# Two weight loads move from SyncE's to ScalarE's DMA queue, and the written-out order of operations is replaced (attention and mixer-MLP layer, one core)

## The chip, the cores and the metric

The kernel runs on one core of a Trainium2 chip. Five engines work side by side, each on its own stream of instructions: TensorE (PE: matrix products and transposes into PSUM; PEld in the profile is its weight load), VectorE (DVE), ScalarE (ACT), GpSimd (POOL) and SyncE (SP, which issues DMAs here). They meet through semaphores. Transfers run on 16 DMA engines.

The metric is the device time of one execution in microseconds. Three runs of the kernel before gave 193.75, 194.11 and 195.71 us; the median is 194.11.

## The reference

The input is x, [1, 2048, 448] in bf16. Two blocks follow one another, each with a residual around it:

```python
h  = x + A_ref(layernorm(x))      # attention, 16 heads of 28
h2 = h + B_ref(layernorm(h))      # token shift + MLP

# A_ref: qkv = x @ wqkv; each position attends to itself and the 7 positions
#   2, 4, ... 14 before it (window 8, dilation 2); softmax; @ wo
# B_ref: h = gelu(layernorm(x) @ w1); its four groups of 112 channels are shifted
#   by +1, -1, +2, -2 positions; hs = shifted @ w2; x1 = x + hs
#   return x1 + gelu(layernorm(x1) @ w3) @ w4        # 448 -> 1792 -> 448
```

## The kernel before, in words

**Tiling.** The 2048 positions are 16 tiles of 128 rows, in xin, one DMA buffer for the whole input. Attention works on four blocks t of 512 positions, the MLP on five units u of 2, 4, 4, 4 and 2 tiles. For a block t the phases are N1 (layernorm), A1 (q and k, transposed to channels x positions), V (values), A2 and S (scores and softmax), A3 and O (weighted sum and wo, with the residual), B1 and M (second layernorm, w1, gelu). For a unit u: B2 (shift and w2) and T (third layernorm), W3 (w3, gelu) and B3 (w4, output). A name such as A11 is phase A1 of block 1.

**Products in pairs.** 448 channels are four chunks that overlap. Most products are made by `duo`, which runs two results at once, one on the upper 64 rows of the array and one on the lower; so the profile has them as 64*128. One operation of the program is such a group of products.

**Layernorm and transposes.** For each tile VectorE makes statistics (bn_stats, bn_aggr into mv), ScalarE or GpSimd makes the reciprocal root (rs_x, then rs_y; `rstd`), and a normalization writes lntm. The transposed lntm, actT, comes from TensorE with copies by ScalarE or VectorE for the attention blocks, and from a transposing DMA on SP for M and W3. The helper chains SP's DMAs around these: a transposing DMA waits for all loads and copies issued since the last one, and the next copies wait for it (`arrange`, lines 205 to 210). For scores, VectorE multiplies q with shifted k into qk_r (phase A2, line 750) and the weights with a mask into bd_r (phase A3); both are long operations on 128x4096 and 80x2048 elements.

**What sets the order.** The program makes 891 operations, numbered as they are made. ORDER (lines 19 to 50) is a permutation of these numbers, written out in the file; each engine's stream is what ORDER has of its operations, in that sequence. The position in ORDER relative to operations of other engines has no effect of its own: semaphores carry the dependences. OTHER lists operations that take their alternative engine (a copy on VectorE for ScalarE or the other way, the product pb in S on GpSimd for VectorE). Waits are made from the dependences (`_emit_plan`); the first goes with the instruction, further ones are instructions of their own (line 992).

**The loads.** `load_x` (lines 428 to 429) and `load_rows` (431 to 434) make the loads; they are operations 8 to 38. All are issued on SP, in the order in which they are made (lines 459 to 462 hold this order per engine). 8, 9 and 10 are the first three loads of x (tile 0, tile 1, tiles 2 and 3); 12 and 13 are the two halves of the q/k part of wqkv, 128 x 2 x 896 elements each, both needed by the first product of A10; 14 and 15 are x tiles 4 to 7; 16 and 17 the v part; 18 and 19 the rest of x; then wo, w1, w2, w3 (35, 36) and w4 (37, 38).

**Operations that the prediction names.** On ScalarE: 60 and 61, 65 and 66, 72 and 73 are the pairs rs_x and rs_y of tile 0, tile 1 and tiles 2 and 3; 11 is a small Exp on a constant, made among the loads (line 440). 101 and 104 are copies of actT in A10, 127 and 134 copies in A10, 230 a copy of actT in A11, 378 one of vt in V2, 408, 528 and 534 copies of actT in A32 and A33, 161 the product pb of S0.

Within a phase the order of instructions on SP before is: x0, x1, x2, wqk (two), x4, x6, wv (two), x8, x12, wo, w1, w2, then copies of vt into vw (V blocks) mixed with w3, transposes for M0 and M1, one vw copy, w4 first half, one vw copy, w4 second half, the transpose for the first W3 unit, two vw copies, the transpose for M2, and so on.

Of the kernel before, what the change touches and what calls it, by code (L numbers as in the profile page):

```python
# [16 lines left out]
POWER = {'N1': 'aaaa', 'B1': 'aaaa', 'B2': 'apapp'}  # L17
RESIDUAL = 'ttvv'
ORDER = """
# [30 lines left out]
"""  # L50
OTHER = """
104 127 196 197 199 402 408 411 519 525 528 582 583
"""
FULL = (4,)
FILL = (1, 1, 0, 0)
# [226 lines left out]
def bass_sequential_preLN__sliding_local_dilated__mixer_s_mlp__prompt_kernel(  # L282
    nc, A_x, A_wqkv, A_wo, B_x, B_w1, B_w2, B_w3, B_w4, out,
):
    _, SEQ, D = A_x.shape
# [30 lines left out]
    with ExitStack() as es:  # L316
# [43 lines left out]
        def arv(off, parts, n):  # L360
            return AR[0:parts, off:off + n]

        wqkv_s = arv(A_W, 128, 4 * 1344).rearrange("p (c n) -> p c n", c=4)
# [29 lines left out]
        def act(out_ap, in_ap, func, **kw):  # L393
            table = {ACT.Exp: "exp", ACT.Ln: "exp", ACT.Gelu_apprx_tanh: "gelu"}.get(func)
            return S.add("act", "activation", table=table, out=out_ap, in_=in_ap, func=func, **kw)
# [15 lines left out]
        def dma(chan, out_ap, in_ap, nbytes, eng="sp", **kw):  # L411
            return S.add(eng, "dma_start", chan=chan, nbytes=nbytes, out=out_ap, in_=in_ap, **kw)
# [15 lines left out]
        def load_x(i, n):  # L428
            return dma("x%d" % i, xin[:, i:i + n, :], xv[:, i:i + n, :], 128 * n * D * 2)

        def load_rows(chan, dst, src, lo, n):

            for h in range(2):
                dma("%s%s" % (chan, "ab"[h]), dst[:, 2 * h:2 * h + 2, :], src[192 * h:192 * h + 256, lo:lo + n].rearrange("(c k) n -> k c n", k=128), 256 * n * 2)

        S.tag = "load"
        for i in range(2):
            load_x(i, 1)
        load_x(2, 2)
        act(zs[:, 0, 0:1], epsilon[:, 0:1], ACT.Exp)  # L440
        load_rows("wqk", wqkv_s[:, :, 0:2 * D], A_wqkv, 0, 2 * D)
        load_x(4, 2)
        load_x(6, 2)
        load_rows("wv", wqkv_s[:, :, 2 * D:3 * D], A_wqkv, 2 * D, D)
        for i in range(8, NTL, 4):
            load_x(i, 4)
# [3 lines left out]
        for k, (to, lo, n) in enumerate(((0, 112, 336), (336, 0, 112), (448, 48, 64))):  # L450
            load_rows("w1%d" % k, w1_s[:, :, to:to + n], B_w1, lo, n)
# [584 lines left out]
```

## Time and profile before

| what | value |
|---|---|
| median of three runs | 194.11 us (193.75 to 195.71) |
| profiled execution: span from its first to its last instruction | 192.0 us |
| the rest of the median, around the span | 2.1 us |
| TensorE busy | 181.2 us, 94% of the span |
| VectorE busy | 129.6 us, 67% |
| ScalarE busy | 133.0 us, 69% |
| GpSimd busy | 29.3 us, 15% |
| TensorE's granted clock | 1.000 |
| 16 DMA engines, hardware queue | 37.1% |

The profiled execution has a span of 192.0 us; what lies around it (launch and end) is not in the span, and is taken as the difference to the median. A line of the profile such as "PE MATMUL ps<-actT,arena 64*128 64x256 bf16 x98" names the engine, the operation, the tile that it writes and those that it reads, its shape and how many there were; all instructions carry line 994, the line that emits them, so one goes by tiles. arena is one large buffer for wqkv, w3, w4, q, k, weights of the attention and the MLP's first result. SPq is SP's queue: a DMA's issue, not its transfer.

### The profile page before, as it was taken

How to read it: one execution, taken by the hardware profiler on the slowest of the kernel's cores; microseconds unless marked ns; L12 is line 12 of the kernel's file. 1: busy time of each engine (PE TensorE's matmuls, PEld its weight loads, DVE VectorE, ACT ScalarE, POOL GpSimd, SP SyncE). 2: the span in 40 equal slices, each digit the busy share in tenths (PEclk: the TensorE clock that was granted, in tenths of full speed). 3: DMA queues.
4: the chain of work that ended last, by engine and by line, in shares of the span. 5: the costliest groups of instructions: out<-in, count | busy, mean ns of one | idle time of the engine just before them, and what ended most of it. 6: DMA issues, size and time to landing. Idle time of an engine off the chain costs nothing.

```text
span 192.0 us, 5741 instructions
## 1 busy us (share of the span) xinstructions
PE 181.2 (94%) x2482; PEld 92.6 (48%) x2482; DVE 129.6 (67%) x229; ACT 133.0 (69%) x310; POOL 29.3 (15%) x63
## 2 busy tenths in 40 slices
PE   6999999999999869969999999999999999999994
PEld 2584533453444333337545444455444544555672
DVE  7899999999999999999876970036988022002203
ACT  4489999999999999998595898860158004731340
POOL 3240000000004000201067000022077700000000
DMA  5998792005504163935905014006200542000111
GB/s 146 353 282 175 194 295 44 14 0 133 133 3 90 23 66 72 319 64 125 113 3 106 8 34 103 0 0 126 58 26 1 109 106 73 0 3 0 51 48 48
DMA packets 30273, 17.04 MB, mean 89 GB/s; under 512 B 18936, under 2 KB 29736, under 8 KB 30248
## 3 DMA queue, kind: packets, MB, share of 16 engines
q1 hardware_dynamic: 30248, 16.68, 37.1%
q8 instruction: 19, 0.31, 0.7%
q14 instruction: 6, 0.05, 0.1%
HBM read 8.04 MB, written 1.84 MB: 51 GB/s over the span
## 4 chain that ended last, share of the span: by engine, by line
PE 67%; DMA 13%; ACT 12%; DVE 3%; SPq 2%; issue 1%; POOL 0%; POOLq 0%; ACTq 0%
PE ps L994 67%; DMA actT<-lntm 7%; DMA arena<-in_B_w_dram 3%; ACT lntm L994 3%; ACT arena L994 3%; DMA vw<-vt 2%; ACT vt L994 2%; SPq L994 2%; DVE bd_r L994 2%; ACT h3T L994 1%; ACT actT L994 1%; ACT xin L994 1%; DVE lntm L994 1%; DVE ost L994 1%; ACT ls L994 1%
## 5 line engine op out<-in xcount | busy, mean ns | idle before, releaser
L994 PE MATMUL ps<-actT,arena 64*128 64x256 bf16 (+1 forms) x756 | 68.7, 329 | 2.2 <-DMA actT<-lntm 1.7
L994 ACT ACTIVATE h3T<-ps 128x512 bf16<-128x512 f32 (+1 forms) x70 | 30.3, 525 | 40.1 <-PE ps L994 40.0
L994 PEld LDWEIGHTS ps<-actT,arena 64*128 64x128 bf16 x756 | 35.4, 94 | 31.6 <-DMA actT<-lntm 2.1
L994 PE MATMUL ps<-arena,h3T 64*128 64x448 bf16 (+2 forms) x434 | 44.4, 343 | 0.0
L994 ACT ACTIVATE arena<-ps 128x512 bf16<-128x512 f32 (+10 forms) x86 | 40.1, 515 | 3.3 <-PE ps L994 2.5
L994 DVE SCALAR_TENSOR_TENSOR ost<-ps,mrs,arena 128x448 bf16<-128x448 f32 (+1 forms) x17 | 10.7, 652 | 36.5 <-PE ps L994 36.5
L994 DVE TENSOR_TENSOR qk_r<-arena 128x4096 bf16<-128x4096 bf16 (+1 forms) x16 | 32.0, 2016 | 0.4 <-ACT arena L994 0.2
L994 PEld LDWEIGHTS ps<-arena,h3T 64*128 64x128 bf16 (+1 forms) x434 | 23.0, 94 | 18.7 <-issue 0.2
L994 POOL TENSOR_TENSOR arena<-arena,xin 128x448 f32<-128x448 f32 x16 | 17.2, 1088 | 45.0 <-DVE lntm L994 45.0
L994 DVE TENSOR_TENSOR bd_r<-arena,bmask 80x2048 bf16<-80x2048 bf16 x16 | 19.0, 1216 | 1.6 <-PE ps L994 0.9
L994 ACT ACTIVATE actT<-ps 128x512 bf16<-128x512 f32 (+2 forms) x21 | 14.6, 742 | 2.1 <-PE ps L994 2.1
L994 PE MATMUL ps<-actT,w_s 64*128 64x512 bf16 x112 | 13.3, 377 | 1.7 <-DMA actT<-lntm 1.2
L994 PE MATMUL ps<-wo_s,actT 64*128 64x448 bf16 x128 | 14.3, 350 | 0.1
L994 PE MATMUL ps<-arena,actT 64*128 64x448 bf16 x112 | 12.4, 350 | 0.4 <-ACT vt L994 0.4
L994 PE MATMUL ps<-w_s,arena 64*128 64x448 bf16 x112 | 11.6, 350 | 1.0 <-ACT arena L994 0.9
L994 ACT ACTIVATE lntm<-xin,nm 128x448 bf16<-128x448 bf16 x16 | 10.5, 660 | 2.6 <-DVE nm L994 2.6
L994 DVE SCALAR_TENSOR_TENSOR arena<-xin,rs_y,ps 128x448 f32<-128x448 bf16 x16 | 10.3, 672 | 2.2 <-PE ps L994 2.2
L994 DVE TENSOR_SCALAR lntm<-arena,mv,rs_y 128x512 bf16<-128x512 f32 x14 | 10.2, 773 | 2.1 <-POOL rs_y L994 2.0
L994 POOL TENSOR_TENSOR pb<-ls,mx 128x512 bf16<-128x512 f32 x2 | 3.3, 1641 | 52.8 <-ACT mx L994 52.8
L994 DVE BATCH_NORM_STATS2 st<-xin 128x6 f32<-128x448 bf16 x16 | 9.4, 614 | 0.8 <-DMA xin<-in_A_x_dram 0.7
L994 PEld LDWEIGHTS ps<-actT,w_s 64*128 64x128 bf16 x112 | 5.1, 94 | 8.9 <-PE ps L994 1.7
L994 PEld LDWEIGHTS ps<-wo_s,actT 64*128 64x128 bf16 x128 | 5.6, 94 | 6.7 <-PE ps L994 1.4
(73 smaller groups left out, 161.7 us busy)
## 6 DMA issues: line engine op xcount, KB each, us to landing
arena<-in_B_w_dram SPq DMA_DIRECT2D x2, 896.0 KB, 7.3
out_dram<-ost SPq DMA_DIRECT2D x15, 112.0 KB, 1.9
arena<-in_B_w_dram SPq DMA_DIRECT2D x2, 784.0 KB, 5.7
vw<-vt SPq DMA_DIRECT2D x4, 320.0 KB, 4.3
vw<-vt SPq DMA_DIRECT2D x4, 256.0 KB, 4.2
arena<-in_A_wqkv_dram SPq DMA_DIRECT2D x2, 448.0 KB, 4.6
xin<-in_A_x_dram SPq DMA_DIRECT2D x2, 448.0 KB, 7.5
xin<-in_A_x_dram SPq DMA_DIRECT2D x3, 224.0 KB, 5.6
```

The lines of the kernel that those rows point to most:

```text
L994: inst = getattr(eng, meth)(**kw)
```

## The change

`load_rows` gets an argument for the issuing engine, and the two loads of the q/k weights (12, 13) pass "act", so they are issued by ScalarE. ORDER is another permutation of the same 891 operations, and OTHER has other members.

```diff
 OTHER = """
-104 127 196 197 199 402 408 411 519 525 528 582 583
+101 134 161 196 197 198 230 378 402 411 519 525 534 582 583
 """
...
-        def load_rows(chan, dst, src, lo, n):
+        def load_rows(chan, dst, src, lo, n, eng="sp"):
 
             for h in range(2):
-                dma("%s%s" % (chan, "ab"[h]), dst[:, 2 * h:2 * h + 2, :], src[192 * h:192 * h + 256, lo:lo + n].rearrange("(c k) n -> k c n", k=128), 256 * n * 2)
+                dma("%s%s" % (chan, "ab"[h]), dst[:, 2 * h:2 * h + 2, :], src[192 * h:192 * h + 256, lo:lo + n].rearrange("(c k) n -> k c n", k=128), 256 * n * 2, eng)
...
-        load_rows("wqk", wqkv_s[:, :, 0:2 * D], A_wqkv, 0, 2 * D)
+        load_rows("wqk", wqkv_s[:, :, 0:2 * D], A_wqkv, 0, 2 * D, "act")
```

Of ORDER, all of which changes, the first three lines before and after:

```diff
-43 8 7 2 11 0 1 49 44 45 6 9 10 12 5 39 13 40 42 58 59 60 61 63 64 62 70 68 50 51 52 53 54 55 56 57 14 65 66 71 69 67
-72 73 75 77 97 15 98 99 100 102 105 74 76 103 101 41 113 119 104 106 46 212 125 218 126 84 107 214 114 216 129 130 215
-89 86 93 78 87 3 108 133 132 115 116 213 217 16 127 128 17 18 219 131 120 109 110 121 338 220 221 224 122 95 223 47
+5 39 6 0 40 1 43 2 42 41 7 8 58 59 60 11 9 63 64 65 10 68 70 69 71 61 62 66 67 72 73 75 44 84 85 92 89 91 74 49 50 51
+52 53 54 55 56 57 97 99 100 102 105 103 12 13 76 98 101 119 106 113 107 77 78 88 46 87 14 214 212 15 218 216 213 217
+47 104 125 120 215 219 220 221 126 129 108 131 130 121 127 128 133 132 122 123 114 124 109 16 17 18 334 223 222 335
...
```

By engine, where the prediction speaks of it:

- ScalarE begins 60, 11, 65, 61, 66, 72, 73, then 12 and 13 (the two loads), then 98 and 106 (copies of actT). Before it began 11, 60, 61, 65, 66, 72, 73, 98.
- VectorE begins with the clearing of vt and pb, both parts of bmask (42, 41), the clearing of wo_s, and then the statistics. Before, it cleared wo_s first and made the second part of bmask after the normalizations of block 0.
- SP issues x0, x1, x2, x4, x6, wv (two), x8, x12, and then a copy of vt of block 0, which has to wait for V0. wo, w1, w2 and w3 come after that.
- Later on SP: transposes for M0 and M1, the two large vw copies of block 3, the transpose for the first W3 unit, w4 (two), one vw copy, the transpose for M2.
- On TensorE all four operations of the first B3 unit stand before M2; before, two of them did, and two came after it, around O3.

54 rows, old and new, of the table ORDER are left out of this document.

## The prediction

> **What bounds the kernel now.** I read the shares of the engines first, then the engines' busy time by stretch, then the chain that ended last and TensorE's own waits, and last the first 16 us instruction by instruction. On the page and in a table of busy time by stretch (columns: length, PE, PEld, DVE, ACT, POOL with instruction counts, clock, DMA share, GB/s):
>
> ```profile
> span 192.0 us, 5741 instructions
> PE 181.2 (94%) x2482; PEld 92.6 (48%) x2482; DVE 129.6 (67%) x229; ACT 133.0 (69%) x310; POOL 29.3 (15%) x63
> 15.60:68.80 53.20, 50.84 (x901) 23.11 (x897) 52.62 (x65) 52.71 (x136) 2.21 (x1) 1.00 0.40 95
> 96.00:188.80 92.80, 92.73 (x983) 48.10 (x984) 37.80 (x83) 46.66 (x93) 19.26 (x21) 1.00 0.19 44
> ```
>
> From 15.6 to 68.8 us (attention) VectorE is busy 52.62 of 53.20 us and ScalarE 52.71: both are full, and whatever arrives late there stays late. From 96 to 188.8 (the MLP) TensorE is busy 92.73 of 92.80 and nothing else matters. So the end is set by when that last, full stretch begins, and by TensorE's gaps before it. The clock is 1.00 throughout. The chain between (start, length, what) and TensorE's waits from 60 to 97 us:
>
> ```profile
> 68.82 5.27 DMA actT<-lntm
> ...
> 76.09 6.49 DMA arena<-in_B_w_dram
> ...
> 82.60 3.06 DMA actT<-lntm
> ...
> 90.60 5.43 DMA actT<-lntm
> ...
> 96.07 92.72 PE ps L994 x981
> ```
> ```profile
> PE ps L994 <- DMA actT<-lntm: 2.9, 3, 1.7
> PE ps L994 <- ACT arena L994: 1.9, 4, 0.7
> PE ps L994 <- ACT rs_x L994: 0.3, 1, 0.3
> ```
>
> The middle is SP's queue in series: transpose for M1 (68.82), then the two w4 loads (to 82.58), then the transpose for the first W3 unit (to 85.67), then two vw copies, then the transpose for M2 (90.60). TensorE waits 5.1 us in all here; the longest wait, 1.7, is for the first W3 unit.
>
> Now the beginning, in order of time:
>
> ```profile
> 0.81 1.34 SPq L994 DMA_DIRECT2D xin<-in_A_x_dram  x3
> 2.19 0.98 SPq L994 DMA_DIRECT2D arena<-in_A_wqkv_dram  x2
> 3.08 0.61 DVE L994 BATCH_NORM_STATS2 st<-xin 128x6 f32<-128x448 bf16 x1
> 6.23 0.30 ACT L994 ACTIVATE rs_x<-mv,epsilon 128x2 f32<-128x2 f32 x1 [1.03 <-DVE mv L994]
> 6.67 1.61 ACT L994 ACTIVATE actT<-ps 128x512 bf16<-128x512 bf16 x3
> 7.42 0.41 DVE L994 TENSOR_REDUCE bmask<-ls 80x32 bf16<-80x256 bf16 x1
> 8.19 5.81 PE L994 MATMUL ps<-actT,arena 64*128 64x256 bf16 x98 [0.24 <-issue]
> 13.84 0.63 PE L994 MATMUL ps<-ident,lntm 64*128 64x64 bf16 x32
> 15.59 2.28 DVE L994 TENSOR_TENSOR qk_r<-arena 128x4096 bf16<-128x4096 bf16 x1
> ```
>
> SP issues the q/k weights at 2.19. The first q/k product starts at 8.19, when the actT copies (6.67 to 8.28) are nearly done as well.
>
> **The change part by part: the loads.** In ScalarE's new order operations 12 and 13 stand behind 60, 11, 65, 61, 66, 72 and 73, that is behind the rs_x row at 6.23 and the rs_y that follows it. Does ScalarE's queue issue a DMA before the instructions ahead of it have been released? The wait instructions (line 992, first and last start at the end of each row) and the landing times bear on it:
>
> ```profile
> L992 PEldq EVENT_SEMAPHORE  x39: 51/51/1280, 7.6 to 182.2; - x39
> L992 POOLq EVENT_SEMAPHORE  x1: 2141/2141/2141, 6.0 to 6.0; - x1
> arena<-in_A_wqkv_dram SPq DMA_DIRECT2D x1, 448.0 KB, 3.8
> arena<-in_A_wqkv_dram SPq DMA_DIRECT2D x2, 448.0 KB, 4.6
> ```
>
> The first half of the weights lands at 2.19 + 3.8 = 6.0, and GpSimd's queue, which has nothing ahead of its wait, shows it at 6.0. (The median of both is 4.6, so the second takes 5.4 and lands at 8.1.) TensorE's queue has transposes ahead of the same wait and comes to it at 7.6 only. So a queue does not pass instructions that are still waiting. I take it that ScalarE's is the same, with DMAs as with waits.
>
> A page of the Trainium skill agrees: PSUM — Partial Sum Buffer, Engine vs sequencer instructions, says that a sequencer waits until prior instructions are dispatched, not until they complete. Another reads differently: Perfetto Trace Analysis, Sequencer Loop, has an engine instruction pushed into a queue in which it waits, while control instructions start at once; by that rule the loads would leave early, which is the second rival below. The 7.6 speaks for the first page.
>
> When is operation 73 released? VectorE's new start is vt, pb, two bmask pieces, then wo_s, then statistics. The second bmask piece (the 0.41 at 7.42) comes ahead of the first statistics and moves them from 3.08 to some 3.3, as part of it falls in idle time; a normalization that stood between the statistics now follows them. The last aggregate still ends at about 6.2, in front of the rs_x row; rs_x (0.30) and the release of rs_y follow, and the two issues run from 6.6 to 7.6 (0.98 for two): 4.4 us later than 2.19.
>
> What is in front of them on the 16 DMA engines? SP no longer stops for the weights, so x and the v weights go out ahead:
>
> ```profile
> xin<-in_A_x_dram SPq DMA_DIRECT2D x2, 448.0 KB, 7.5
> xin<-in_A_x_dram SPq DMA_DIRECT2D x3, 224.0 KB, 5.6
> arena<-in_A_wqkv_dram SPq DMA_DIRECT2D x2, 224.0 KB, 5.8
> xin<-in_A_x_dram SPq DMA_DIRECT2D x2, 112.0 KB, 2.1
> 1.60:7.20 5.60, 5.47 (x19) 2.26 (x19) 4.93 (x16) 2.62 (x10) 0.90 (x5) 1.00 0.92 271
> 7.20:12.00 4.80, 4.50 (x75) 3.59 (x76) 3.96 (x12) 2.65 (x10) 3.59 (x25) 1.00 1.09 362
> ```
>
> That is 896 + 672 + 448 + 224 = 2240 KB, plus 896 of q/k weights: 3136 KB, or 3211 thousand bytes. By 7.2 some 271 x 5.6 = 1518 are moved; the other 1693 at 362 GB/s take 4.7 us, to 11.9. The second load now lands 1.4 after its bytes are through by the same count (448 + 896 KB are 1376 thousand bytes, at 7.2 - 142/271 = 6.7; it lands at 8.1), with other loads pressing from behind; now SP stalls behind x, nothing presses, and between 0 and 1.4 I take 0.4: 12.3. The row of the second load gives the same, 7.1 + 5.4 = 12.5. Bounds: 10.5, if ScalarE's queue were served first (7.6 + 918/362 + 0.4), and 13.3 with the whole lag. I take **12.3**, against 8.1: TensorE's first product moves by **+4.2** (+2.4 to +5.2).
>
> The skill has a rule against the change as such. DMA: Bandwidth & Descriptors, Issuing engines are not separate DMA queues, says that DMAs of different engines share the same 16 DMA engines, so a second issuer saves issue time only; the share of 1.09 at 362 GB/s agrees. By it an early issue would save at most the 1.34 us that SP needs for the x loads in front.
>
> **What the delay does.** The transposes of the second block (13.84 + 0.63) end 6.3 us after the first product starts, now at 18.7. VectorE has done its statistics by then and idles. Its copy of actT (operation 230, new on VectorE: 0.42 is the row for half its size, so 0.85) and two aggregates follow; the first qk_r product starts at about 19.9 instead of 15.59: **+4.3**. From there VectorE is full, so the 4.3 reach 68.8 whole; its idle 0.58 in that stretch could give back 0 to 0.6, and I take 0.
>
> **The moved operations.** 101, 134, 230, 378 and 534 go to VectorE, 104, 127, 408 and 528 to ScalarE, 161 to GpSimd:
>
> ```profile
> L994 DVE TENSOR_TENSOR pb<-ls,mx x2: 679/682/684, 32.5 to 47.3; 128x512 bf16<-128x512 f32 x2
> L994 POOL TENSOR_TENSOR pb<-ls,mx x2: 1075/1641/2207, 60.0 to 86.1; 128x512 bf16<-128x512 f32 x2
> 7.99 0.42 DVE L994 COPY actT<-ps 128x512 bf16<-128x512 bf16 x1 [0.17 <-PE ps L994]
> ```
>
> VectorE loses 0.68 (161) and four copies and gains five; the nearest row for a copy is 0.42, twice that for the wide one: even within 0.7 us, and I take 0. GpSimd's pb takes 1.64, 1.0 more, ahead of the S0 transposes; TensorE, which has idle room there behind the full engines, hides it; uncovered it costs 1.0. Two table loads of ScalarE fewer fall behind 96 us, where it isn't the bound: 0.
>
> **The middle.** SP's new order puts the two big vw copies, not the w4 loads, between the transposes for M1 and the first W3 unit, and w4 after it. All shifted by 4.3: M1's transpose lands at 78.4, the copies (issued in about 1 us, as any two of SP's, and landing 4.3 after) at 83.2 to 83.7, the transpose of 3.06 could be in at 86.8 or, if normalization sets it, 87.7:
>
> ```profile
> 79.35 1.00 DVE L994 TENSOR_SCALAR lntm<-arena,nm,rs_y 128x512 bf16<-128x512 f32 x2
> vw<-vt SPq DMA_DIRECT2D x4, 320.0 KB, 4.3
> 80.98 3.06 PE L994 MATMUL ps<-w_s,arena 64*128 64x448 bf16 x28 [0.23 <-ACT arena L994]
> 85.71 3.47 PE L994 MATMUL ps<-actT,arena 64*128 64x256 bf16 x56 [1.66 <-DMA actT<-lntm]
> 89.49 2.58 PE L994 MATMUL ps<-actT,arena 64*128 64x256 bf16 x42
> 91.91 2.81 PE L994 MATMUL ps<-arena,h3T 64*128 64x448 bf16 x28
> ```
>
> (Normalization now ends at 80.35 + 4.3 + 3.06 = 87.7.) TensorE itself finishes the products before it at 84.04 + 4.3 = 88.3. So its 1.66 of waiting go, and W3 starts at 88.3. W4, issued from 87.7, lands at about 87.7 + 0.5 + 6.5 = 94.7, when the 6.1 us of W3 (3.47 + 2.58) have just been done; all four parts of the first B3 (twice the 2.81 row, which is two of them) now stand before M2. M2's transpose (5.43) follows w4 at 100.1, and TensorE has B3 until 94.7 + 5.6 = 100.3: covered, so the short wait in front of 96.07 (0.4, what is left of 2.9 after the 1.7 and the 0.8 for M0) goes too. Given back: 1.66 + 0.4 = 2.1. **Sum:** +4.3 - 2.1 = +2.2: a span of 194.2 and, as the span is 2.1 below the median of the runs (194.11), **196.3**.
>
> **The rivals.** (1) *Nothing is given back*, since w4, now late, holds up the first B3 as the W3 transpose was held up, or pb on GpSimd is uncovered: +4.3 to +5.3, 198.4 to 199.4. For it: w4 and W3 come out within half a microsecond of each other, and M2's transpose and B3 too. Against: TensorE's gap of 1.66 is in the way of nothing else. (2) *ScalarE's queue runs ahead of its waits* and issues at about 2.3. Then the weights share the engines with x from about 3 us: at most 1.4 x 271 = 380 thousand bytes are moved by then, and as many of x as of weights until these are done, 2216 in all; 7.2 + (2216 - 1518)/362 = 9.1, and 10.5 with the lag. That is +1.0 to +2.4 at the start, less 2.1: 193.0 to 194.4, no difference. (3) *Not slower, and perhaps faster:* the loads are late but the order dissolves all 5.1 us of TensorE's waits after 60. With +4.3 that is -0.8, 193.3; with the weights landing at 10.5 it is 2.4 - 5.1 = -2.7, 191.4. It decides for faster when the landing is below some 11.2 and all the waits go. Against: 2.2 of the waits are for ScalarE, which is full up to there. (4) *The change does nothing*, as another load binds the first product: it can't be, as 12 and 13 are needed whole by it.
>
> **How the numbers follow.** A measurement of this kernel tells about 1%, 1.9 us, from no change: slower means over 196.05, faster under 192.2. My forecast (195.1 to 197.8) has 0.47, two thirds of it above 196.05; rival 1 has 0.24; rival 2 has 0.10; rival 3 has 0.19, of which 0.13 under 192.2. Together slower 0.55, same 0.32, faster 0.13. The range takes in rivals 1 and 2 and the end of 3 that loses nothing: 193.0 to 199.6.
>
> **What would show it.** ScalarE's queue shows two DMA issues at 6.6 to 7.6 (rival 2: 2 to 3). GpSimd's wait for the weights ends at about 12.3, and TensorE's first 64x256 products start there. The first 128x4096 qk_r product starts near 19.9, M1's transpose near 73.1, the first W3 product at about 88, and the last full stretch of TensorE has no gap before M2. A landing below 11, or TensorE with none of its waits after 60, would make me wrong on the fast side; a wait of TensorE for arena<-in_B_w_dram on the slow side.

## The result, and the profile after

The changed kernel takes 205.30 us (median of four runs, 203.86 to 206.26), the kernel before 194.06 beside it: a ratio of 1.055, with a 95% interval of 1.048 to 1.062. It is slower by 11.2 us, where 2.2 were forecast. The profiled execution took 204.83 us, with a span of 203.1.

On the page of the changed kernel, the span and the slices of TensorE's granted clock (40 slices of 5.1 us, in tenths, 9 is full):

```profile
span 203.1 us, 5745 instructions
PEclk9966999999999998799999999999999999999999
```

The clock is the first surprise: it is down in the third and fourth slice (10 to 20 us) and again in the 16th and 17th (76 to 86). In the kernel before it was 1.00 in every stretch that was read. That is its one profiled execution, though. Of 52 later executions of the kernel before, 35 had a mean granted clock of 0.982 to 0.991, which is about what one or two stretches of 3.4 us at half clock make of a span of 192 us; where they lay was not traced. These 35 took 194.46 us in the median (193.53 to 196.07), the other 17, at 0.999 and above, 194.04 (193.21 to 194.86).

The start of the changed kernel in order of time:

```profile
6.30 0.20 ACT L994 ACTIVATE rs_y<-rs_x 128x2 f32<-128x2 f32 x1
6.31 0.95 ACTq L994 DMA_DIRECT2D arena<-in_A_wqkv_dram  x2
...
13.40 0.74 POOL L994 COPY arena<-arena 128x256 bf16<-128x256 bf16 x2 [5.58 <-DMA arena<-in_A_wqkv_dram]
...
13.60 7.70 PE L994 MATMUL ps<-actT,arena 64*128 64x256 bf16 x92 [5.50 <-DVE mv L994]
...
23.21 2.29 DVE L994 TENSOR_TENSOR qk_r<-arena 128x4096 bf16<-128x4096 bf16 x1 [0.23 <-ACT arena L994]
```

ScalarE's queue issues the two loads 0.01 us after rs_y (operation 73) is released. GpSimd's wait for the weights ends at 13.40 and TensorE starts at 13.60 (the profile names a VectorE aggregate as the releaser, but these products do not read mv; the weights came last). Then 92 products take 7.70 us, and qk_r starts at 23.21 instead of 15.59: 7.6 us late, not 4.3.

The same kernel by stretch (columns as in the prediction: length, PE, PEld, DVE, ACT, POOL, then clock, DMA share and GB/s):

```profile
0.00:7.20 7.20, 4.68 (x20) 1.96 (x21) 6.04 (x17) 2.70 (x8) 1.63 (x12) 1.00 0.69 190
...
10.80:12.00 1.20, 0.00 (x0) 0.00 (x0) 1.11 (x5) 0.20 (x1) 0.00 (x0) 0.98 0.97 370
12.00:12.60 0.60, 0.00 (x0) 0.00 (x0) 0.60 (x3) 0.00 (x0) 0.00 (x0) 0.50 0.39 149
12.60:13.40 0.80, 0.00 (x0) 0.00 (x0) 0.80 (x2) 0.00 (x0) 0.00 (x0) 0.50 0.03 11
...
13.60:18.40 4.80, 4.80 (x46) 3.85 (x48) 0.47 (x1) 0.00 (x0) 2.73 (x18) 0.50 0.00 0
18.40:23.20 4.80, 4.80 (x102) 4.04 (x99) 0.84 (x3) 4.38 (x13) 0.00 (x0) 0.96 0.02 3
...
76.40:79.90 3.50, 0.48 (x40) 0.33 (x36) 3.50 (x7) 3.38 (x7) 0.00 (x0) 1.00 0.33 39
...
80.20:83.60 3.40, 3.40 (x52) 1.36 (x48) 1.65 (x2) 3.32 (x7) 0.00 (x0) 0.50 0.76 118
```

TensorE does nothing from 8.1 on; from 12.0 the clock is 0.50, and it stays there until 18.4, although TensorE is at work from 13.6: 46 products in the 4.8 us before 18.4, 102 (shorter transposes among them) in the 4.8 us behind it. In the middle the same happens after a stretch in which TensorE was not idle but nearly so (0.48 of 3.50 us). The old order had gaps at this place too, in the same work, but TensorE was busy for half of the time, and the clock held:

```profile
66.80:70.20 3.40, 1.70 (x104) 0.97 (x100) 3.40 (x7) 3.30 (x7) 0.00 (x0) 1.00 0.05 9
```

TensorE's waits from 60 to 100 us, the one that comes after 100, and the end of the chain, of the changed kernel:

```profile
PE ps L994 <- ACT arena L994: 4.6, 3, 1.9
PE ps L994 <- ACT h3T L994: 0.9, 1, 0.9
```
```profile
PE ps L994 <- DMA actT<-lntm: 0.9, 1, 0.9
```
```profile
142.90 4.27 DMA actT<-lntm
147.21 52.65 PE ps L994 x553
```

From 60 to 100 us the transposing DMA no longer tops TensorE's waits (2.9 us before). ScalarE does, with 4.6 us in three waits, where the kernel before had 1.9 in four: 3.5 in front of B2 of the first two units (1.93 and 1.54) and 1.1 in front of a group of A3 products. One wait for a transposing DMA is new, in front of 147.2. From there on TensorE is full again, and everything is 11.1 us later than before.

### The profile page after: what moved, and what is told of

It is laid out like the page before. It is cut to its first block, busy times and chain, and to the rows that moved or that the text cites. A ratio compares the mean times of both kernels' runs of the same rounds, so it can differ in the third digit from the quotient of the medians.

```text
span 203.1 us, 5745 instructions
## 1 busy us (share of the span) xinstructions
PE 183.1 (90%) x2482; PEld 95.4 (47%) x2482; DVE 129.3 (64%) x229; ACT 131.4 (65%) x307; POOL 31.6 (16%) x64
## 3 DMA queue, kind: packets, MB, share of 16 engines
HBM read 8.04 MB, written 1.84 MB: 49 GB/s over the span
## 4 chain that ended last, share of the span: by engine, by line
PE 58%; ACT 30%; DVE 6%; DMA 2%; issue 1%; POOL 1%; ACTq 0%
PE ps L994 58%; ACT arena L994 13%; ACT lntm L994 5%; ACT actT L994 3%; DVE st L994 3%; ACT vt L994 2%; DMA actT<-lntm 2%; ACT xin L994 2%; DVE lntm L994 1%; ACT L994 1%; POOL pb L994 1%; ACT ls L994 1%; ACT L989 1%; ACT mx L994 1%; DVE ost L994 1%
## 5 line engine op out<-in xcount | busy, mean ns | idle before, releaser
L994 PE MATMUL ps<-actT,arena 64*128 64x512 bf16 (+1 forms) x756 | 71.0, 338 | 7.3 <-DVE mv L994 5.5
L994 PEld LDWEIGHTS ps<-actT,arena 64*128 64x128 bf16 x756 | 37.6, 97 | 37.0 <-DVE mv L994 5.6
L994 ACT ACTIVATE arena<-ps 128x512 bf16<-128x512 f32 (+9 forms) x87 | 41.1, 508 | 10.4 <-PE ps L994 9.2
L994 DVE SCALAR_TENSOR_TENSOR ost<-ps,mrs,arena 128x448 bf16<-128x448 f32 (+1 forms) x17 | 10.8, 653 | 36.2 <-PE ps L994 32.2
L994 ACT ACTIVATE actT<-ps 128x512 bf16<-128x512 f32 (+2 forms) x21 | 13.9, 699 | 7.0 <-PE ps L994 7.0
L994 DVE TENSOR_SCALAR lntm<-arena,mv,rs_y 128x512 bf16<-128x512 f32 x14 | 9.1, 694 | 11.3 <-ACT rs_y L994 9.4
L994 PE MATMUL ps<-w_s,arena 64*128 64x448 bf16 x112 | 12.9, 371 | 3.5 <-ACT arena L994 3.5
L994 PE MATMUL ps<-wo_s,actT 64*128 64x448 bf16 x128 | 14.8, 357 | 0.5 <-ACT actT L994 0.4
L994 PE MATMUL ps<-actT,w_s 64*128 64x512 bf16 x112 | 13.6, 377 | 0.1
L994 POOL TENSOR_TENSOR pb<-ls,mx 128x512 bf16<-128x512 f32 x3 | 4.8, 1596 | 56.5 <-ACT mx L994 56.5
L994 ACT ACTIVATE lntm<-xin,nm 128x448 bf16<-128x448 bf16 x16 | 10.5, 662 | 0.0
L994 PEld LDWEIGHTS ps<-wo_s,actT 64*128 64x128 bf16 x128 | 6.1, 97 | 7.4 <-issue 2.2
L994 PEld LDWEIGHTS ps<-w_s,arena 64*128 64x128 bf16 x112 | 5.3, 97 | 8.9 <-ACT arena L994 4.2
```

The source lines that it names most:

```text
L994: inst = getattr(eng, meth)(**kw)
```

## The experiments

Three theories were in play. One: the late place of the loads in ScalarE's stream is the whole loss, with what it sets off. Two: the new order costs something of its own. Three: TensorE's clock, and not the waits alone, is a part of both. (Where the expectations count the steps of the prediction, step 2 is what stands in front of the weights, step 4 the moved operations and step 5 the middle.)

### Where the loads are issued, and the order without them

The new order with the loads early on ScalarE (of ORDER, the entries that move):

```diff
-... 42 41 7 8 58 59 60 11 9 63 64 ... 102 105 103 12 13 76 98 ...
+... 42 41 7 8 11 12 13 58 59 60 9 63 64 ... 102 105 103 76 98 ...
```

> The changed kernel with operations 11, 12 and 13 at the head of ScalarE's stream: the same queue and the same order otherwise, only issued early. After the change TensorE's first q/k product came 5.4 us later than before and the first qk_r product 7.6 later, and the end 11.1 later. Theory A (the late place in ScalarE's stream, with all that it sets off, is the whole loss): the weights land at about 9.1 to 10.5 as I had worked out for an early issue, first qk_r at 16.5 to 18, time 194.5 to 197. Theory B (the late place costs the 7.6 and the new order costs the other 3.5 by itself, in the middle): 198 to 200. Theory C (ScalarE's queue as such is slow to deliver, wherever it is issued): landing above 11 again, time over 201.

The new order with the loads on SP again:

```diff
-        load_rows("wqk", wqkv_s[:, :, 0:2 * D], A_wqkv, 0, 2 * D, "act")
+        load_rows("wqk", wqkv_s[:, :, 0:2 * D], A_wqkv, 0, 2 * D)
```

> The changed kernel with the two q/k loads back on SP between x2 and x4, as before the change: the new order alone. Theory A: the first q/k product at 8.2 as before, time 194 to 195.5, no difference from the kernel before. Theory B: start as before and 3.5 lost after it, 197 to 198.5. Against the early issue on ScalarE, SP's is 0.9 to 2.4 faster if x in front of the weights on the shared DMA engines is what counts, and equal if not.

The old order with the loads on ScalarE, early, is the kernel before with the two code lines of the change and nothing of its ORDER:

> The kernel before with the two loads on ScalarE, where its old order has them: at the head of ScalarE's stream. The queue alone. Priced from the shared DMA engines: landing at 9.1 to 10.5 against 8.1, +1.0 to +2.4, time 195 to 196.5. If two queues help (SP's issue of x4 onwards and the weights go side by side and the weights start earlier), 193 to 194.

The same with the loads late:

```diff
-... 9 10 12 5 39 13 40 42 ... 69 67 72 73 75 77 ...
+... 9 10 5 39 40 42 ... 69 67 72 73 12 13 75 77 ...
```

> The kernel before with the two loads on ScalarE behind operation 73, the place that they have after the change, all else in the old order. Theory A: first q/k product at about 13.6, TensorE idle for 5 us, granted clock down to about 0.54 to 0.74 in the 9 us behind it, time 203 to 206, most of the loss with nothing of the new order. Theory B: 200.5 to 202.5. If my +4.3 for the start were right after all and the clock had nothing to do with it: 198 to 199.

| kernel | us | ratio to before (95%) |
|---|---|---|
| new order, ScalarE, early | 199.38 | 1.026 (1.021 to 1.031) |
| new order, SP | 198.15 | 1.020 (1.016 to 1.024) |
| old order, ScalarE, early | 197.78 | 1.018 (1.013 to 1.022) |
| old order, ScalarE, late | 205.48 | 1.055 (1.049 to 1.060) |

Theory B holds for the order: with the loads where they were, it still costs 3.7 us. The queue as such does not help either: early on ScalarE is 1.2 us worse than SP in the new order (198.54 to 200.59 against 197.67 to 198.94) and 3.3 worse than SP in the old one, more than I expected. One reason shows in the timelines. First the new order, with a row of its stretches, then the old, with the loads early on ScalarE:

```profile
1.89 0.42 ACTq L994 DMA_DIRECT2D arena<-in_A_wqkv_dram  x1
...
6.48 1.15 DVE L994 BATCH_NORM_STATS2 st<-xin 128x6 f32<-128x448 bf16 x2 [1.64 <-DMA xin<-in_A_x_dram]
...
10.22 6.20 PE L994 MATMUL ps<-actT,arena 64*128 64x256 bf16 x92
```
```profile
9.60:10.80 1.20, 1.20 (x13) 0.84 (x12) 1.20 (x3) 0.90 (x2) 1.20 (x9) 0.50 1.10 375
```
```profile
6.79 1.15 DVE L994 BATCH_NORM_STATS2 st<-xin 128x6 f32<-128x448 bf16 x2 [0.71 <-DMA xin<-in_A_x_dram]
...
9.86 2.40 PE L994 MATMUL ps<-actT,arena 64*128 64x256 bf16 x22
```

Now x is late: the statistics of tiles 2 and 3, which in the changed kernel run without a wait, stand until 6.5 or 6.8 for a load that shares the DMA engines with the weights. The first product follows at 9.9 to 10.2, not for the weights but for x. This is what the Trainium skill says in DMA: Bandwidth & Descriptors, Issuing engines are not separate DMA queues, and the runs agree: the second issuer saved nothing here, and x came late.

The clock is a part of these two times as well. TensorE stood idle for 2.5 us in the new order and 1.5 in the old while it waited for x, and the granted clock was 0.50 from 9.0 to 12.3 and from 10.0 to 13.4: in the new order the 92 products take 6.20 us instead of the 5.20 with the loads on SP. No run holds the clock here, so how much of the 1.2 and 3.3 us is x and how much the clock stays open.

The late place in the old order:

```profile
6.61 0.94 ACTq L994 DMA_DIRECT2D arena<-in_A_wqkv_dram  x2
...
16.74 0.61 PE L994 MATMUL ps<-actT,arena 64*128 64x256 bf16 x4 [8.74 <-DMA arena<-in_A_wqkv_dram]
```

The total is what theory A gave, but by another mixture, with the first product at 16.7 where 13.6 was expected: the loads were issued 0.3 us later than in the changed kernel and TensorE got them 3.1 later, since SP's old order sends wo and w1 right behind x and the new one stops there. What the old order loses more at the start it loses less behind it.

### What stands in front of the weights

In this kernel x4, x6, the v weights, x8 and x12 go on ScalarE too, behind the weights:

```diff
-        load_x(4, 2)
-        load_x(6, 2)
-        load_rows("wv", wqkv_s[:, :, 2 * D:3 * D], A_wqkv, 2 * D, D)
+        load_x(4, 2, "act")
+        load_x(6, 2, "act")
+        load_rows("wv", wqkv_s[:, :, 2 * D:3 * D], A_wqkv, 2 * D, D, "act")
         for i in range(8, NTL, 4):
-            load_x(i, 4)
+            load_x(i, 4, "act")
```

> The changed kernel with the loads x4, x6, the v weights, x8 and x12 on ScalarE too, behind the q/k weights, so that SP has nothing but x0 to x2 in front of them (everything that needs those later loads comes late, so only the start is read). If the weights wait for the x and v loads on the shared DMA engines (step 2 of the prediction): issued at 6.3 to 7.3 as before and landed by 10.0 to 10.8, against 13.4. If the landing is the queue's own 6 us and not the neighbours' bytes: 13 again.

The start in order of time:

```profile
6.24 0.95 ACTq L994 DMA_DIRECT2D arena<-in_A_wqkv_dram  x2
...
7.98 0.90 ACTq L994 DMA_DIRECT2D xin<-in_A_x_dram  x2
...
11.01 0.74 POOL L994 COPY arena<-arena 128x256 bf16<-128x256 bf16 x2 [3.26 <-DMA arena<-in_A_wqkv_dram]
...
11.21 3.04 PE L994 MATMUL ps<-actT,arena 64*128 64x256 bf16 x28 [3.05 <-DMA arena<-in_A_wqkv_dram]
```

The same issue time, and GpSimd sees the weights at 11.0 instead of 13.4, and that with x4 and x6 still issued 1.7 us behind them. So 2.4 us of the landing are the neighbours' bytes, as the prediction had it; 11.0 against 10.0 to 10.8 is a small miss. (The whole takes 216.56 us in its single run, as its later x comes late.)

### The clock at the start

Twenty-four products that nobody reads are put into TensorE's wait in the changed kernel:

```diff
+        S.tag = "fill"
+        for n in (24,):
+            mms([(busy(), ident[:], bass.AP(ident, 0, [[128, 128], [0, 4], [1, 128]]), True, True, 512, None)] * n)
...
-... 103 12 13 76 98 101 119 ...
+... 103 12 13 76 98 101 891 119 ...
```

> The changed kernel with 24 products of ident with itself (128x512, into the bank of the warm-up, read by nobody) put into TensorE's stream in front of the first q/k product, so that TensorE is busy for some 5 us of the wait for the weights; all else unchanged. After the change the granted clock stood at 0.50 from 12.0 to 18.4 us, and the first 92 q/k products took 7.70 us instead of the 5.20 that they took with the loads on SP. Theory A (the clock falls because TensorE idles from 8.1 to 13.6): the clock stays at 1.00 in 8 to 20 us, the 92 products take 5.2 to 5.8, first qk_r at 21.3 to 21.8 instead of 23.2, time 203.4 to 204.0 against 205.3. Theory B (the late evictions on ScalarE, not the clock, set the pace of these products): qk_r at 23.0 to 23.3, time 205.0 to 205.5.

In its timeline (the line that emits is 998 here, as four were added above it):

```profile
7.92 5.34 PE L998 MATMUL ps<-ident 128*128 128x512 bf16 x24
13.72 5.20 PE L998 MATMUL ps<-actT,arena 64*128 64x256 bf16 x92 [0.45 <-DVE mv L998]
...
20.92 2.29 DVE L998 TENSOR_TENSOR qk_r<-arena 128x4096 bf16<-128x4096 bf16 x1 [0.33 <-ACT arena L998]
```

202.66 us against 205.30: 2.6 us less, for doing more. The weights land no earlier (13.72), but the 92 products take 5.20 us, and qk_r comes 2.3 us earlier. Theory A is shown, and it was more than expected. The order with the loads on SP has the same 5.20 and its qk_r at 16.27, in its timeline:

```profile
8.26 5.20 PE L994 MATMUL ps<-actT,arena 64*128 64x256 bf16 x92 [0.19 <-ACT actT L994]
...
16.27 2.29 DVE L994 TENSOR_TENSOR qk_r<-arena 128x4096 bf16<-128x4096 bf16 x1
```

With the clock held at the start, then, lateness alone is 4.65 us at qk_r (20.92 against 16.27) and 4.51 in the times (202.66 against 198.15). Both kernels still have the low clock in the middle.

### The clock in the middle

The new order with the loads on SP and seven such products, in a bank of their own, in front of the first B2 product:

```diff
-... 211 210 500 413 414 572 417 ...
+... 211 210 500 413 414 891 572 417 ...
```

> The new order with the q/k loads on SP (the run of 198.15 us), with 7 products of ident with itself in front of the first B2 product of the middle, in a bank of their own: at full clock 1.5 us of work in a wait of 1.93 for ScalarE's gelu. There the new order had TensorE idle for 1.09 and 1.93 us within 3.4, and the granted clock was 0.50 for the 3.3 us behind it (73.7 to 77.0), which the old order never had. Theory A (the new order pays for the middle twice, once for the wait and once for the clock): the clock stays 1.00 in 73 to 77, time 196.4 to 197.2. Theory B (only the waits count, what follows is set by ScalarE and VectorE): 198.0 to 198.4.

By stretch, without the seven products and then, for the second of the two stretches, with them:

```profile
70.10:73.50 3.40, 0.42 (x32) 0.30 (x32) 3.40 (x7) 3.28 (x7) 0.00 (x0) 1.00 0.25 37
73.50:77.00 3.50, 3.48 (x48) 1.46 (x50) 1.57 (x2) 3.47 (x6) 0.00 (x0) 0.53 1.07 121
```
```profile
73.50:77.00 3.50, 3.50 (x68) 1.46 (x70) 2.93 (x7) 3.47 (x8) 0.00 (x0) 1.00 0.80 116
```

196.31 us (195.26 to 197.97), 1.84 less: half of what the new order costs is this one dip of the clock. In the 3.5 us behind the wait TensorE does 68 products instead of 48. Six of the seven executions have a mean granted clock of 0.999 or more; the seventh, at 0.991, is the one of 197.97. What is left against the kernel before is a ratio of 1.009 (1.004 to 1.014).

### The two halves of the order

One kernel has the old order up to the first M0 product (405 entries) and the new one for all that is left; the other has the new one up to there (427 entries) and the old one after it. Both have the loads on SP.

> Old order up to the first M0 product, new order for all that is left, q/k loads on SP: the old attention with the new middle and MLP. The new order whole (loads on SP) costs 3.75 us; 1.84 of it is the clock in the middle. Theory A (the middle is the whole loss): 197.5 to 198.5. Theory B (attention loses what is left of it, about 1.9, and the middle only its clock and waits): 195.8 to 197.0. If the low clock needs the attention of the new order, the clock stays 1.00 and the time is 194 to 195.

> New order up to the first M0 product, old order for all that is left, q/k loads on SP: the new attention with the old middle and MLP. Theory A (attention loses nothing): 194.0 to 194.8. Theory B (VectorE's waits in the new attention, 2.5 us against 0.4, cost their difference): 195.8 to 196.6, and no low clock in the middle. Both halves should sum to about 3.75 over the kernel before.

They take 196.68 us (ratio 1.012, 1.008 to 1.017) and 197.29 (1.015, 1.006 to 1.023). The halves do not sum to 3.75: they make 2.5 and 3.1 over the kernel before in their runs. The first is in the range of its theory B. The second is above both of its theories, and it has the low clock that it was not to have. I had not thought of the seam. It lies in front of B2, where TensorE's longest wait is now 2.9 us in both kernels (1.9 in the whole new order, 0.7 in the old), and by stretch both (first the new middle, then the new attention) have the dip there:

```profile
69.10:72.10 3.00, 0.05 (x6) 0.03 (x4) 3.00 (x5) 2.90 (x6) 0.00 (x0) 1.00 0.34 68
72.10:75.50 3.40, 3.40 (x52) 1.50 (x54) 1.72 (x2) 3.19 (x6) 0.00 (x0) 0.60 0.52 101
```
```profile
72.80:76.20 3.40, 3.33 (x22) 1.16 (x22) 2.22 (x4) 2.62 (x4) 0.00 (x0) 0.62 0.75 118
```

So a third kernel: the old attention with the new middle, and 11 products in that wait (operation 891 in front of 572, as above).

> Old attention with the new middle and MLP (196.68 us) and 11 products of ident with itself in front of the first B2 product, where TensorE waits 2.95 us for ScalarE's gelu: 2.4 us of work at full clock. Both halves of the two orders, put together either way, had that wait and the clock at 0.50 behind it. Theory A (the new middle costs its clock and little else): clock 1.00 in 72 to 76, time 194.5 to 195.2, within 0.5% of the kernel before. Theory B (its waits for ScalarE cost by themselves): 196.0 to 196.7. Were it under 193.5, it would beat both kernels.

194.79 us beside 194.54 of the kernel before: a ratio of 1.0015 (0.998 to 1.005). In the stretch behind the wait the clock holds:

```profile
73.50:77.00 3.50, 3.50 (x42) 1.42 (x38) 3.02 (x6) 3.04 (x9) 0.00 (x0) 1.00 0.30 80
```

Beside the median of the kernel before, the new middle costs its clock and no more. That comparison flatters it: all twelve executions had a mean clock of 0.998 or more, and only five of the 17 of the kernel before beside them. Those five took 193.80 in the median (193.21 to 194.72), so with the clock held on both sides the new middle is some 1.0 us slower. The kernel before was not run with such products.

This run also prices the new attention. It differs from the run of 196.31 us in the order up to the first M0 product alone (and in 11 products for 7), with the clock held in both: 196.31 against 194.79 is about 1.5 us. The two were measured in different sets, and the intervals of their ratios just touch.

### The part that was to give something back

The kernel before, with SP's and TensorE's steps of the middle close to what the new order has, and nothing else. (Not quite as the new order has them: there two further vw copies, 501 and 504, come after w4, and a part of A33 stands between the two halves of B3.)

```diff
 SP:  ... vwc1 (504)
-     w4 (37)  vwp1 (501)  w4 (38)  transpose (586)  vwb1 (503)  vwa1 (502)  transpose (440)
+     vwp1 (501)  vwb1 (503)  vwa1 (502)  transpose (586)  w4 (37)  w4 (38)  transpose (440)
 PE:
-     B30 (615, 616)  A33  M2 (447, 441, 448, 442)  A33  B30 (617)  O3  B30 (618)
+     B30 (615, 616, 617, 618)  A33  M2 (447, 441, 448, 442)  A33  O3
```

> The kernel before with the one part of the new order from which I had expected a gain: SP issues the last vw copies and the transpose for the first W3 unit ahead of both w4 loads, and TensorE has all four B3 operations of the first unit in front of M2. Loads of q/k on SP as before, all else in the old order. By step 5 of the prediction TensorE's wait of 1.66 for that transpose and the 0.43 in front of M2 go: 1.7 to 2.1 less, 192.3 to 192.8. Rival 1 (w4, now late, holds up the first B3 instead): 194.0 to 194.8, no difference, with a wait of TensorE for arena<-in_B_w_dram.

TensorE in order of time:

```profile
83.82 1.03 PE L994 MATMUL ps<-actT,arena 64*128 64x256 bf16 x16
85.57 2.60 PE L994 MATMUL ps<-actT,arena 64*128 64x256 bf16 x40 [0.71 <-DVE arena L994]
...
91.09 5.70 PE L994 MATMUL ps<-arena,h3T 64*128 64x448 bf16 x56
96.72 1.00 PE L994 MATMUL ps<-bd_r,vw 80*32 80x64 bf16 x96
97.65 3.19 PE L994 MATMUL ps<-actT,w_s 64*128 64x512 bf16 x28
...
103.05 3.20 PE L994 MATMUL ps<-wo_s,actT 64*128 64x448 bf16 x32 [1.86 <-DVE actT L994]
```

196.00 us, a ratio of 1.010 (1.005 to 1.014): neither the 192.3 to 192.8 of step 5 nor the no difference of rival 1. (The six executions with a mean clock of 1.000 took 195.66 in the median, so it isn't the clock.) The wait of 1.66 for the transpose does go (W3 starts at 83.82 instead of 85.71) and the one in front of M2 too, though W3 now waits 0.71 for VectorE, and by B3 0.82 of the gain is left (91.09 against 91.91). But A33 and M2 now stand behind 5.70 us of B3 and begin at 96.72 and 97.65 instead of 94.65 and 96.07, and the O3 products wait 1.86 us for VectorE's copy of A33's result. The same stretch of the kernel before:

```profile
94.65 0.99 PE L994 MATMUL ps<-bd_r,vw 80*32 80x64 bf16 x96
96.07 3.20 PE L994 MATMUL ps<-actT,w_s 64*128 64x512 bf16 x28 [0.43 <-DMA actT<-lntm]
...
99.55 1.50 PE L994 MATMUL ps<-arena,h3T 64*128 64x448 bf16 x14
...
104.02 1.49 PE L994 MATMUL ps<-arena,h3T 64*128 64x448 bf16 x14
```

There the two B3 operations behind M2 (1.50 at 99.55, 1.49 at 104.02) are what TensorE does while VectorE copies. They had been cover, and I took them from where they covered. In the changed kernel, where a part of A33 comes before the second half of B3, this wait does not occur; so this run shows what the part does in the old order, and not what became of it in the new one.

### The product pb

```diff
-101 134 161 196 197 198 230 378 402 411 519 525 534 582 583
+101 134 196 197 198 230 378 402 411 519 525 534 582 583
```

> The new order with the q/k loads on SP (198.15 us), with operation 161 (the product pb of S0) back on VectorE, all else as it is. By step 4 of the prediction GpSimd's pb is hidden: no difference, 198.0 to 198.4. If the extra 1.0 to 1.3 us of pb on GpSimd lies on the path (the chain of waits after the change runs through it for 1.97 us, and TensorE waits for it twice, 1.1 us in all): 197.0 to 197.5. If VectorE, which gets 0.68 more, is the tighter: 198.6 to 198.9.

199.37 us against 198.15: not faster, so no cost of pb on GpSimd is seen; the time is above all three forecasts. Whether putting it back costs 1.2 us isn't settled: in its profiled execution 0.87 us are lost already in front of the first q/k product (8.26 with 161 on GpSimd), where the two kernels are the same:

```profile
9.13 6.02 PE L994 MATMUL ps<-actT,arena 64*128 64x256 bf16 x92
```

TensorE is slower there: between 9 and 11 us it does 26 products, against 45 with 161 on GpSimd, with a granted clock of 1.00 in both traces. qk_r starts 0.89 us later for it (17.16 against 16.27), which is most of the 1.2. So in the first microseconds the clock column does not tell the whole pace; why they differ stays open.

No kernel of these beat the one before.

## Why the prediction was wrong, point by point

The medians split the loss: 3.7 us for the new order with the loads on SP (198.15 over 194.45), of which 1.84 are the clock in the middle and about 1.5 the new attention; 4.5 for the late weights with the clock held at the start; 2.6 for the clock at the start. That is 10.8 of 11.2; the kernel before was at 194.06 and 194.45 in the two sets of runs, which is the rest. That it would be slower was forecast as the likeliest case (0.55), but the largest terms of the loss were not in the sum.

- **ScalarE's queue does not pass instructions that wait**: right. The loads were issued at 6.31 to 7.26 (forecast 6.6 to 7.6), on the release of 73. Rival 2, which would have had them at 2 to 3, is refuted.
- **The weights land at 12.3** (10.5 to 13.3): 13.4, just outside; the mechanism was right and the size off by 1.1. The bytes were through at 12.6, not 11.9: by 7.2 us 190 x 7.2 = 1368 thousand were moved, not 1518, which is 0.4 us of it at the later rate. And they were seen at 13.4, a lag of 0.8 where I took 0.4.
- **The first qk_r at 19.9** (+4.3): 23.21. This is the first step that failed. It carried the 6.3 us between the first product and the end of the second block's transposes over from the old profile, at a clock of 1.00, into a kernel in which TensorE stands still for 5.5 us before. With the clock held there, qk_r came at 20.92, so 2.3 of the 3.3 us missed are the clock; the 1.0 that is left is about what the landing was late.
- **From there the shift stays whole**: right for the delay. With the clock held at the start it was 4.65 us at qk_r and 4.51 in the times. But the new order adds to it on the way: the transpose for M1 was issued at 78.07, where 73.1 was forecast.
- **The moved operations cost 0**: this failed too. No run shows a cost for 161. But I priced operations one by one and not the order in which they now stand. With the loads on SP, VectorE has 2.5 us without work (54.83 less 52.34) in the new attention, from the first qk_r on, where the old one had 0.6 in its 53.20:

```profile
16.27:71.10 54.83, 50.38 (x903) 23.89 (x899) 52.34 (x61) 53.08 (x134) 4.79 (x5) 1.00 0.43 106
```

  With the clock held and the same new middle, the new attention cost 1.5 us (196.31 against 194.79). That VectorE's idle time is the cause is likely, as it is about as long, but no run shows it.
- **The middle gives back 2.1**: the step that failed most. Together with the moved operations the new order was forecast at -2.1 and measured at +3.7, a miss of 5.8 us; of this the middle gave back nothing and cost the 1.84 of its clock. The wait that it named does go. TensorE's timeline of the changed kernel has the second unit's B2 and the first unit's W3 at

```profile
92.72 2.82 PE L994 MATMUL ps<-w_s,arena 64*128 64x448 bf16 x28 [1.54 <-ACT arena L994]
95.38 3.54 PE L994 MATMUL ps<-actT,arena 64*128 64x256 bf16 x56
```

  which is 11.74 us behind the old one for B2 (80.98) and 9.67 for W3 (85.71): 2.07 given back, at that place. But I listed only the waits that would go and not the new ones: 3.5 us for ScalarE in front of both units' B2 (1.54 of it in the first row) where the old order had 0.9, the low clock behind the first of them, 0.9 inside W3, and 0.9 for a transposing DMA in front of 147.2. The last two, less the 0.4 in front of M2 that went, bring the 9.67 back to about the 11.1 of the end.
- **The rivals**: rival 1 (nothing given back) was the right one of the four and gave 198.4 to 199.4, far too little, since none had a clock in it.

The rule of the page that bears on this stands in the Trainium skill, TensorE: Matmul & The Clock Gate, What's actually happening: the array's clock is halved after an idle window of about 3.4 us and released by activity. The runs agree on the half (0.50) and on the length (nearly idle from 70.1, halved behind 73.5). They add that TensorE needn't be idle all that time: with 0.42 of 3.40 us busy the clock fell. No safe share can be read from them: in the profiled execution of the kernel before it held with 1.70 of 3.40 us busy, and in the old order with the loads early on ScalarE it fell with 1.76 of the last 3.40 us busy.

## What to carry to other kernels

A clock of 1.00 in the old profile belongs to that one execution of the old order, and not to the operations: before a wait on TensorE is priced at its length, look how much of the 3 to 4 us around it TensorE is busy, and where it is little, add the half-speed work behind it, or fill the wait with products that nobody reads. A DMA moved to ScalarE's queue was issued here behind every wait ahead of it, so its place in that engine's stream set its issue time. And where a reorder takes work out of one gap to close another, name the gap that it had been filling.

## What the runs showed of the hardware

- TensorE's clock fell to 0.50 some 3.3 to 4 us after TensorE had gone quiet (8.1 to 12.0, 70.1 to 73.7; 5.7 to 9.0 with the loads early in the new order, although TensorE was at work again from 8.2). It came back 3.5 to 5.3 us after TensorE was busy again (73.5 to 77.0, 13.6 to 18.4; 16.7 to 22.0 with the late loads in the old order). The dip cost 1.8 us in the middle of the new order and 2.6 at the start of the changed kernel; adding work took both away.
- Two loads issued on ScalarE at nearly the same time (6.24, 6.31 and 6.61) were waited for until 11.0, 13.4 and 16.7 us, by how much SP had issued in front of and beside them.
